# One load and product for v of four heads, f32 dummy matmuls, and batch 1's scores from pair 0 on

## The chip, the core and the metric

The kernel runs on one core of a Trainium2 chip. The core has a matrix engine (PE, with its weight loads listed as PEld), a vector engine (DVE), an activation engine (ACT), a general engine (POOL) that here issues the loads from memory, and a queue engine (SP) that here issues DMA transposes and stores. Matrix products go to an accumulation memory of eight banks, from which DVE and ACT copy them out. The metric is the time of one execution on the device in microseconds (us); the median of four runs stands for the kernel.

## The reference

Eight batches of eight heads, 1024 positions, 64 numbers a head. Keys and values are projected along the positions to 64 rows, then come attention over these 64 rows and a two-layer network on the result:

```python
k_proj = np.einsum('ks,bhsd->bhkd', E, k)
v_proj = np.einsum('ks,bhsd->bhkd', F, v)
scores = scale * np.matmul(q, k_proj.transpose(0, 1, 3, 2))
attn = softmax(scores)
x = np.matmul(attn, v_proj)            # (8, 8, 1024, 64) -> rows of 512
h = x @ w_in                           # 512 -> 2048
g = h * np.clip(h + 3.0, 0.0, 6.0) / 6.0
out = g @ w_out                        # 2048 -> 512, 8192 rows
```

All inputs and the output are f32 in memory; the kernel computes with bf16 operands and f32 sums.

## The kernel before

The program is written with its order by hand: each engine runs its instructions in the order in which the code issues them.

**Tiling.** Tokens are taken in blocks of 512 (TOK), two to a batch. Heads go in pairs j = 0 to 3: a pair is 128 columns of the model's 512. The first layer's 2048 columns are 16 groups of 128 (fo), each with four products of 128 rows (ko = the pair j), and the second layer accumulates 16 products into one output tile of 128 rows.

**PSUM tiles.** Two pools of four banks: `pmm()` and `pat()`. Each call takes the next of its four buffers, and the writer waits until the buffer's former reader is done.

**Start.** E and F come in over SP and ACT, are cast on DVE (L140) and ACT (L141), turned by eight PE transposes (L145) and copied to `e_t` and `f_t` (L147, L149). Meanwhile PE runs dummy matmuls on a constant tile of ones: `busy(n)` (L86 to L89) issues n matmuls of 128x512 bf16, into a `pmm` tile that nobody reads. There are 12 at the start (L91), two after the transposes (L151), and single ones inside the first block (L464, L467, L476). The tile `ones` also serves as the stationary operand of the sums of softmax (L255, L431).

**Loads of batch 0.** POOL issues them in this order, with a cast from f32 to bf16 on the way: four times a pair of k and half of a pair of q; then v in four loads of a pair (L113); then w_in in eight pieces (L127 to L129), the rest of q, w_out, and batch 1's k, v and q. They all go through one queue. A load waits for the load eight places before it in the list.

**First block (class First, L437 to L480).** For each pair j: `keys(j)` projects k with eight matmuls and copies the result to `kp` on DVE; `queries` transposes q; `scores(j - 1)` multiplies q and the keys of the pair before, and ACT takes the exponential (L445, one instruction for each head of the pair); `keys_transposed(j)` turns kp on PE; `sums(j)` multiplies the exponentials by ones, and ACT turns the result into 1/sum as exp(-ln) (L450, L451). `vals(j)` projects v of pair j with eight matmuls of 128 columns, and DVE (ACT for the last) copies the result to `vp` (L394). `products(j)` multiplies the weights of softmax by vp, and DVE scales the result by 1/sum into xT (L454), the first layer's input. The loop ends with pair 3's `keys_transposed`; the order behind it is lines 468 to 480: scores of pair 3, vals 0, sums 2, vals 1, products 0, sums 3, vals 2, products 1, one dummy, products 2, vals 3, then `meanwhile`, which is the first product with w_in (L169), and products 3. Then the dense work on both layers begins.

**Batch 1 (class Attention).** Its projection runs on PE at 56 us, DVE copies the keys to kp (L205), SP issues one DMA transpose of the keys to kT (L212) and two of q to qT (L157): the first fills pairs 0 and 1, the second pairs 2 and 3. A copy of one element, `mark` (L219), lets POOL go on to the next batch's loads when the first of them has landed. `visit(n)` (L332 to L361) is called for n = 0 to 3 among the groups of the second layer of batch 0's second block. `visit(0)` issues the scores of three pairs in the order 2, 0, 1 (L334), the first into two pmm tiles and the others into pat tiles, then their exponentials on ACT in the same order. `visit(1)` issues sums and values of pair 0 and the scores of pair 3; `visit(2)` sums and values of pair 1 and the sums of pair 2; `visit(3)` the rest.

From then on PE alternates between the groups of the two layers, with the attention of later batches spread among them.

Of the kernel before, what the change touches and what calls it, by code (L numbers as in the profile page):

```python
# [8 lines left out]
f32 = mybir.dt.float32  # L9
bf16 = mybir.dt.bfloat16  # L10
# [5 lines left out]
def kernel(  # L16
# [11 lines left out]
    nc = tc.nc  # L28
# [5 lines left out]
    P = 128  # L34
    SO = S // P
    KO = d_model // P
    FO = d_ff // P
    TOK = 512
# [13 lines left out]
    consts = ctx.enter_context(tc.tile_pool(name="consts", bufs=1))  # L52
# [13 lines left out]
    def pmm():  # L66
        return ps_mm.tile([P, TOK], f32, tag="mm", name="mm")

    def pat():
        return ps_at.tile([P, TOK], f32, tag="at", name="at")  # L70
# [7 lines left out]
    nc.sync.dma_start(out=ef_f32[:KP], in_=E)  # L78
    nc.scalar.dma_start(out=ef_f32[KP:], in_=F)
    nc.scalar.preload_act_table_set("natural_log_exp_and_others")  # L80
    ones = consts.tile([P, TOK], bf16, name="ones")
    nc.vector.memset(ones, 1.0)  # L82
    ident = consts.tile([P, P], bf16, name="ident")


    def busy(n):  # L86
        ps = pmm()
        for _ in range(n):
            nc.tensor.matmul(ps, ones[:, :P], ones, start=True, stop=True)  # L89

    busy(12)  # L91

    def raw_tile(name):
        return kqv_pool.tile([P, H, SO, D], bf16, tag=name, name=name)


    kqv = {0: {n: raw_tile(n) for n in ("k", "q", "v")}}
# [3 lines left out]
    def load_q0(t, hs):  # L101
        nc.gpsimd.dma_start(out=q0[:, t, hs], in_=kqv_dram["q"][0][:, hs, t * SB:(t + 1) * SB, :])  # L102

    def load_pair(n, j):
        hs = slice(2 * j, 2 * j + 2)
        nc.gpsimd.dma_start(out=kqv[0][n][:, hs], in_=kqv_dram[n][0][:, hs])  # L106

    for j in range(KO):
        load_pair("k", j)
        load_q0(0, slice(2 * j, 2 * j + 2))  # L110
        if j == 0:
            make_identity(nc, ident)
    for j in range(KO):  # L113
        load_pair("v", j)

    def load_kqv(b, order="qkv"):
        kqv[b] = {}
# [20 lines left out]
    f_t = consts.tile([P, SO, 2, KP], bf16, name="f_t")  # L138
# [9 lines left out]
    for a in range(2):  # L148
        nc.scalar.copy(f_t[:, :, a, :], ef_pv[:, 1])  # L149
    ef_t = [e_t, f_t[:, :, 0, :]]  # L150
    busy(2)  # L151

    def q_transposed(b):
# [17 lines left out]
    def rec_tile():  # L171
        return att.tile([P, 2, TOK], f32, tag="rec", name="rec", bufs=4)

    def log(rec, i, den):
        nc.scalar.activation(rec[:, i], den, AF.Ln)

    def inverse(rec, den=()):
        for i, d in enumerate(den):
            log(rec, i, d)
        flat = rec.rearrange("p i n -> p (i n)")  # L180
        nc.scalar.activation(flat, flat, AF.Exp, scale=-1.0)  # L181
# [5 lines left out]
    class Attention:  # L187
# [143 lines left out]

        def visit(self, n):  # L332
            if n == 0:
                js = 2, 0, 1  # L334
                tiles = [self.scores(j, *two) for j, two in zip(js, ((pmm, pmm), (pat, pat), (pat, pat)))]
                for j, two in zip(js, tiles):
                    self.exps(j, two)
                return lambda: None
            if n == 1:
                den, av = self.sums(0, pmm, pmm), self.values(0, pat, pat)  # L340
                last = self.scores(3, pat, pat)
                rec = rec_tile()
                inverse(rec, den)
                self.exps(3, last)
                return lambda: self.scaled(0, av, rec)
            if n == 2:
                den, av = self.sums(1, pmm, pmm), self.values(1, pat, pat)
                more = self.sums(2, pat, pat)
                rec, self.rec = rec_tile(), rec_tile()
                inverse(rec, den)  # L350
                later.extend([lambda i=i: log(self.rec, i, more[i]) for i in range(NB)])
                later.append(lambda: inverse(self.rec))
                return lambda: self.scaled(1, av, rec)
            den = self.sums(3, pmm, pat)
            early = self.values(2, pmm, pmm)
            av = self.values(3, pat, pat)
            rec = rec_tile()
            inverse(rec, den)
            self.scaled(2, early, self.rec)
            return lambda: self.scaled(3, av, rec)  # L360
# [3 lines left out]
    class First:  # L364
# [20 lines left out]
                                    self.kp[:, 2 * j + a].rearrange("p a d -> p (a d)"), ident[:KP, :KP])  # L385
            nc.vector.tensor_copy(self.kT[:, 2 * j:2 * j + 2, :].rearrange("p h m -> p (h m)"), ps)

        def vals(self, j, copy):
            ps = pat()[:, :P]
            for so in range(SO):  # L390
                nc.tensor.matmul(ps, f_t[:, so].rearrange("p a m -> p (a m)"),
                                 kqv[0]["v"][:, 2 * j:2 * j + 2, so, :],
                                 start=(so == 0), stop=(so == SO - 1))
            copy(self.vp[:, 2 * j:2 * j + 2, :].rearrange("p h d -> p (h d)"), ps)  # L394

        def queries(self, t, js):

# [39 lines left out]
        def first_block(self, meanwhile):  # L437
            recs = {}

            def scores(j):  # L440
                aT = att.tile([P, 2, HT], bf16, tag="aT0", name="aT0", bufs=KO)
                tiles = [pmm() for _ in range(2)]
                self.scores(0, j, tiles, 0)
                for r in range(2):
                    nc.scalar.activation(aT[:, r], tiles[r][:, :HT], AF.Exp, scale=scale)  # L445
                self.aT[0, j] = aT

            def sums(j):
                recs[j] = opool.tile([P, TOK], f32, tag="o_sb", name="o_sb")
                nc.scalar.activation(recs[j], self.sums(0, j, pmm), AF.Ln)  # L450
                nc.scalar.activation(recs[j], recs[j], AF.Exp, scale=-1.0)  # L451

            def products(j):
                nc.vector.tensor_mul(self.xT[:, j, 0, :], self.values(0, j, pat), recs[j])  # L454

            for j in range(KO):
                self.keys(j)
                if j > 1:
                    sums(j - 2)
                self.queries(0, (j,))  # L460
                if j > 0:
                    scores(j - 1)
                else:
                    busy(1)  # L464
                self.keys_transposed(j)
                if j < 2:
                    busy(1)  # L467
            scores(KO - 1)
            self.vals(0, nc.vector.tensor_copy)
            sums(KO - 2)  # L470
            self.vals(1, nc.vector.tensor_copy)
            products(0)
            sums(KO - 1)
            self.vals(2, nc.vector.tensor_copy)
            products(1)
            busy(1)  # L476
            products(2)
            self.vals(3, nc.scalar.copy)
            meanwhile()
            products(3)  # L480
# [103 lines left out]
    def meanwhile():  # L584
        early.append(TwoGroups(xT, 0, g[0]))
        early[0].part(0, (0,))
# [48 lines left out]
    for b in range(1, B):  # L635
# [6 lines left out]
        two, more = ((pmm, pmm), (pat, pat)), (pat, pat)  # L642
# [29 lines left out]
        for t in range(NB):  # L672
            g = g_tile()
            for fo in range(FO):
# [13 lines left out]
                n = t * SB + slots.index(fo)  # L688
# [43 lines left out]
```

## Time and profile before

| | us |
|---|---|
| median of four runs | 503.11 |
| lowest and highest | 502.77, 503.64 |
| the profiled execution's own time | 502.77 |
| its span, first to last instruction | 501.0 |
| PE busy | 494.6 |
| DVE busy | 285.3 |
| ACT busy | 239.5 |
| POOL busy | 38.7 |
| POOL's issues of v, four of them, from 7.57 | 2.91 in all |
| first issue of w_in | 10.68 |
| first product with w_in | 20.09 |

The span lies within the execution's own time; what lies around it is 502.77 - 501.0 = 1.77 us.

In an excerpt in order of time, a line gives the start, the length, the engine, the line of code, the operation, what it writes and reads, the form (partitions x elements) and, after x, how many instructions are merged into it; the square brackets give the idle time of the engine just before, and what ended it. Matmuls overlap: a new one starts before the end of the former one, so the distance of the starts is the cost of one, not its length. In a list of waits a line gives who waited for whom, the sum in us, the number of times and the longest.

### The profile page before, as it was taken

To read this page: it belongs to the slowest core of one execution; us is meant where nothing else is said; L and a number is where in the kernel's file an instruction comes from. 1 tells how busy PE (TensorE), PEld (TensorE's weight loads), DVE (VectorE), ACT (ScalarE), POOL (GpSimd) and SP (SyncE) were. 2 spreads that over 40 slices of the span, in tenths; PEclk is the share of its full clock that TensorE was granted. 3 is DMA by queue.
4 is the path that set the end of the run, shared out by engine and by line. 5 is a ranking of instruction groups with operands and counts; after the bars stand their busy time and mean duration, and the time that the engine had idled before them with its cause. 6 is when DMAs were issued, how large, how long until landed. Compare 5 with 4: busy or idle time off the path is not lost.

```text
span 501.0 us, 11177 instructions
## 1 busy us (share of the span) xinstructions
PE 494.6 (99%) x4802; PEld 256.1 (51%) x4802; DVE 285.3 (57%) x438; ACT 239.5 (48%) x414; POOL 38.7 (8%) x58
## 2 busy tenths in 40 slices
PE   8999999999999999999999999999999999999997
PEld 4554544554555545555555545555455554555554
DVE  3572736876658675666648655674755656334420
ACT  3656566665355445433564344643456344343431
POOL 8620020200020020002000020000000000000000
PEclk9999999999999999999999999999999999999999
DMA  9999999898759799549950799209411261101112
GB/s 168 198 204 207 187 174 231 150 210 176 175 95 222 174 191 215 112 113 225 207 122 22 178 195 223 73 24 232 116 43 44 59 176 44 43 22 43 44 43 84
DMA packets 83618, 68.43 MB, mean 137 GB/s; under 512 B 38256, under 2 KB 69232, under 8 KB 83568
## 3 DMA queue, kind: packets, MB, share of 16 engines
q0 software_dynamic: 32480, 29.36, 37.5%
q1 hardware_dynamic: 50864, 38.02, 30.9%
q8 instruction: 37, 0.61, 0.5%
q10 hardware_dynamic: 224, 0.33, 0.3%
q14 instruction: 13, 0.11, 0.1%
HBM read 71.83 MB, written 16.97 MB: 177 GB/s over the span
## 4 chain that ended last, share of the span: by engine, by line
PE 91%; DMA 5%; POOL 2%; SPq 1%; issue 0%; ACT 0%; DVE 0%; ACTq 0%; POOLq 0%
PE mm L169 85%; DMA qT<-q 3%; PE at L169 2%; DMA w_in_sb<-in_moe_w_in_dram 2%; PE mm L250 1%; PE at L229 1%; PE at L250 1%; PE mm L229 1%; POOL q L102 1%; POOL v L106 1%; POOL k L106 1%; SPq L212 0%; SPq L157 0%; PE at L425 0%; PE at L405 0%
## 5 line engine op out<-in xcount | busy, mean ns | idle before, releaser
L514 DVE SCALAR_TENSOR_TENSOR g<-r,mm 128x512 bf16<-128x512 f32 x256 | 174.3, 687 | 143.6 <-ACT r L513 142.9
L169 PE MATMUL mm<-w_out_sb,g 128*64 128x512 bf16 (+2 forms) x2080 | 235.6, 376 | 0.0
L169 PE MATMUL mm<-xT,w_in_sb 128*64 128x512 bf16 x2048 | 231.1, 379 | 0.2 <-DMA w_in_sb<-in_moe_w_in_dram 0.2
L513 ACT ACTIVATE r<-mm 128x512 f32<-128x512 f32 x256 | 152.7, 598 | 74.5 <-PE mm L169 73.3
L169 PEld LDWEIGHTS <-w_in_sb 128*64 128x64 bf16 x2048 | 115.7, 110 | 105.1 <-issue 0.6
L169 PEld LDWEIGHTS <-g 128*64 128x64 bf16 x2080 | 114.8, 110 | 106.5 <-issue 7.1
L548 ACT COPY o_sb<-mm 128x512 f32<-128x512 f32 x58 | 33.9, 585 | 149.9 <-PE mm L169 149.5
L270 DVE TRANSPOSE_TENSOR_REDUCE parts<-aT 128x32 f32<-128x1024 bf16 x24 | 28.8, 1226 | 0.0
L262 DVE TENSOR_TENSOR xT<-at,rec 128x512 bf16<-128x512 f32 x32 | 20.5, 683 | 8.6 <-ACT rec L181 5.8
L238 ACT ACTIVATE aT<-at 128x512 bf16<-128x512 f32 x38 | 20.7, 622 | 7.9 <-PE at L229 7.9
L262 DVE TENSOR_TENSOR xT<-mm,rec 128x512 bf16<-128x512 f32 x24 | 15.5, 686 | 7.3 <-PE mm L250 7.2
L219 POOL COPY mark<-qT 1x1 bf16<-1x1 bf16 x5 | 0.9, 177 | 202.4 <-DMA qT<-q 202.4
L205 DVE CAST kp<-at 64x512 bf16<-64x512 f32 x14 | 9.0, 678 | 11.3 <-PE at L169 11.2
L238 ACT ACTIVATE aT<-mm 128x512 bf16<-128x512 f32 x18 | 9.7, 605 | 7.6 <-PE mm L229 7.6
L169 PE MATMUL at<-k,e_t 128*64 128x512 bf16 x56 | 13.2, 379 | 0.0
L169 PE MATMUL at<-v,f_t 128*64 128x512 bf16 x56 | 13.2, 379 | 0.0
L208 DVE CAST vp<-at 64x512 bf16<-64x512 f32 x14 | 9.7, 694 | 0.4
L538 DVE COPY o_sb<-mm 128x384 f32<-128x384 f32 x1 | 0.6, 558 | 15.2 <-PE mm L169 15.2
L169 PEld LDWEIGHTS <-e_t 128*64 128x64 bf16 x56 | 6.2, 110 | 5.7
L89 PE MATMUL mm<-ones 128*128 128x512 bf16 x18 | 7.4, 549 | 1.5 <-DVE ones L82 1.5
L229 PEld LDWEIGHTS <-kT 64*64 64x64 bf16 x224 | 5.7, 106 | 5.2 <-issue 4.3
L503 DVE TENSOR_TENSOR xT<-at,rec 128x512 bf16<-128x512 f32 x4 | 2.5, 684 | 8.1 <-PE at L425 8.1
(68 smaller groups left out, 152.0 us busy)
## 6 DMA issues: line engine op xcount, KB each, us to landing
out_dram<-o_sb SPq DMA_DIRECT2D x63, 256.0 KB, 4.4
rec<-turned_rows SPq DMA_DIRECT2D x48, 256.0 KB, 6.4
k<-in_k_dram POOLq DMA_DIRECT2D x7, 1024.0 KB, 10.7
v<-in_v_dram POOLq DMA_DIRECT2D x7, 1024.0 KB, 15.7
q<-in_q_dram POOLq DMA_DIRECT2D x7, 1024.0 KB, 20.5
w_out_sb<-in_moe_w_out_dram POOLq DMA_DIRECT2D x4, 512.0 KB, 16.0
w_in_sb<-in_moe_w_in_dram POOLq DMA_DIRECT2D x5, 256.0 KB, 9.9
k<-in_k_dram POOLq DMA_DIRECT2D x4, 256.0 KB, 5.4
```

Source lines behind the costliest of these rows:

```text
L106: nc.gpsimd.dma_start(out=kqv[0][n][:, hs], in_=kqv_dram[n][0][:, hs])
L169: nc.tensor.matmul(ps[lo:lo + width], stationary[:, lo:lo + width], moving, **flags)
L205: nc.vector.tensor_copy(self.kp[:, :, a, :], self.ps[:KP].rearrange("p (h d) -> p h d", d=D))
L208: nc.vector.tensor_copy(self.vp[a * KP:(a + 1) * KP], self.ps[KP:].rearrange("p (h d) -> p h d", d=D))
L229: nc.tensor.matmul(tiles[r][t * KP:(t + 1) * KP, a * HT:(a + 1) * HT], self.kT[r * D:(r + 1) * D, 2 * j + a, :], qT[r * D:(r + 1) * D, j, ...
L238: when(lambda r=r: nc.scalar.activation(aT[:, :, r, :], tiles[r].rearrange("p (a n) -> p a n", a=2), AF.Exp, scale=scale))
L250: nc.tensor.matmul(tiles[t][c:c + D], stationary(r, 2 * j + a), self.weights(j, a)[r:r + KP], start=True, stop=True)
L262: when(lambda t=t: nc.vector.tensor_mul(self.xT[:, j, t, :], av[t], rec[:, t]))
L270: nc.vector.tensor_reduce(out=self.parts[:, j], op=ALU.add, axis=mybir.AxisListType.X, apply_transpose=True, in_=self.aT[j].rearrange("p a ...
L513: nc.scalar.activation(r, h_ps, AF.Relu, bias=0.5, scale=1.0 / 6.0)
L514: nc.vector.scalar_tensor_tensor(g[:, fo, :], r, 1.0, h_ps, op0=ALU.min, op1=ALU.mult)
L548: (copy or nc.scalar.copy)(o_sb, o_ps)
```

## The change

Four edits, in the order of the code.

1. `ones` is filled as 128x256 f32 with a number whose two halves are both the bf16 number 1; the bf16 tile `ones` is the same bytes, read as 128x512 bf16.
2. `busy(n)` multiplies f32 columns, 128 for each of the n of before, at most 256 in one matmul: `busy(12)` issues six of 256, `busy(2)` one of 256, `busy(1)` one of 128. In the instruction order an f32 matmul has no weight load of its own in front of it.
3. v of batch 0's pairs 0 and 1 comes in one load, and `vals` takes `more` pairs: `vals(0, ..., 2)` projects both pairs with eight matmuls of 256 columns and one copy. The order around it becomes: scores of pair 3, sums 2, vals 0 and 1, sums 3, products 0, vals 2, and on as before.
4. `visit(0)` scores the pairs in the order 0, 1, 2.

```diff
-    ones = consts.tile([P, TOK], bf16, name="ones")
-    nc.vector.memset(ones, 1.0)
+    ones_f32 = consts.tile([P, TOK // 2], f32, name="ones")
+    nc.vector.memset(ones_f32, 1.0 + 127 * 2.0 ** -16)
+    ones = ones_f32.bitcast(bf16)
...
     def busy(n):
         ps = pmm()
-        for _ in range(n):
-            nc.tensor.matmul(ps, ones[:, :P], ones, start=True, stop=True)
+        for lo in range(0, n * P, 2 * P):
+            m = min(2 * P, n * P - lo)
+            nc.tensor.matmul(ps[:, :m], ones_f32[:, :P], ones_f32[:, :m], start=True, stop=True)
...
-    def load_pair(n, j):
-        hs = slice(2 * j, 2 * j + 2)
+    def load_pairs(n, j, more=1):
+        hs = slice(2 * j, 2 * (j + more))
         nc.gpsimd.dma_start(out=kqv[0][n][:, hs], in_=kqv_dram[n][0][:, hs])
...
-    for j in range(KO):
-        load_pair("v", j)
+    load_pairs("v", 0, 2)
+    for j in range(2, KO):
+        load_pairs("v", j)
...
             if n == 0:
-                js = 2, 0, 1
+                js = 0, 1, 2
...
-        def vals(self, j, copy):
-            ps = pat()[:, :P]
+        def vals(self, j, copy, more=1):
+            hs = slice(2 * j, 2 * (j + more))
+            ps = pat()[:, :more * P]
             for so in range(SO):
-                nc.tensor.matmul(ps, f_t[:, so].rearrange("p a m -> p (a m)"),
-                                 kqv[0]["v"][:, 2 * j:2 * j + 2, so, :],
+                nc.tensor.matmul(ps, f_t[:, so].rearrange("p a m -> p (a m)"), kqv[0]["v"][:, hs, so, :],
                                  start=(so == 0), stop=(so == SO - 1))
-            copy(self.vp[:, 2 * j:2 * j + 2, :].rearrange("p h d -> p (h d)"), ps)
+            copy(self.vp[:, hs, :].rearrange("p h d -> p (h d)"), ps)
...
             scores(KO - 1)
-            self.vals(0, nc.vector.tensor_copy)
             sums(KO - 2)
-            self.vals(1, nc.vector.tensor_copy)
+            self.vals(0, nc.vector.tensor_copy, 2)
+            sums(KO - 1)
             products(0)
-            sums(KO - 1)
             self.vals(2, nc.vector.tensor_copy)
```

More of the change, by code (lines that the diff above doesn't have):

```diff
@@ L102, in load_q0 @@
         nc.gpsimd.dma_start(out=q0[:, t, hs], in_=kqv_dram["q"][0][:, hs, t * SB:(t + 1) * SB, :])
-    def load_pair(n, j):
-        hs = slice(2 * j, 2 * j + 2)
+    def load_pairs(n, j, more=1):
+        hs = slice(2 * j, 2 * (j + more))
         nc.gpsimd.dma_start(out=kqv[0][n][:, hs], in_=kqv_dram[n][0][:, hs])
     for j in range(KO):
-        load_pair("k", j)
+        load_pairs("k", j)
         load_q0(0, slice(2 * j, 2 * j + 2))
```

## The prediction

> **What bounds the kernel now.** I read the busy times first, then the list of what PE waited for, then PE, ACT and POOL in order of time over the first 21 us, and last the stretch around 69 us. The page's first part and PE's whole list of waits:
>
> ```profile
> PE 494.6 (99%) x4802; PEld 256.1 (51%) x4802; DVE 285.3 (57%) x438; ACT 239.5 (48%) x414; POOL 38.7 (8%) x58
> ...
> PE mm L89 <- DVE ones L82: 1.5, 1, 1.5
> PE mm L425 <- ACT aT L445: 0.6, 1, 0.6
> PE mm L229 <- DMA qT<-q: 0.4, 1, 0.4
> PE mm L418 <- DVE kT L386: 0.3, 1, 0.3
> PE mm L169 <- DMA w_in_sb<-in_moe_w_in_dram: 0.2, 1, 0.2
> ```
>
> PE is the bound: 494.6 of 501.0 us. All five waits lie before 70 us. After that PE runs without a hole, so a delay or gain of PE before 70 us arrives at the end unchanged. The change touches that stretch at two places: the first 20 us, and the wait for qT. The first, in order of time on PE:
>
> ```profile
> 1.46 5.30 PE L89 MATMUL mm<-ones 128*128 128x512 bf16 x12 [1.46 <-DVE ones L82]
> 6.55 0.86 PE L145 MATMUL at<-ident,g 128*128 128x128 bf16 x8
> 7.25 0.59 PE L89 MATMUL mm<-ones 128*128 128x512 bf16 x2
> 7.93 0.63 PE L375 MATMUL at<-k,e_t 128*64 128x128 bf16 x8
> ...
> 15.62 0.30 PE L418 MATMUL mm<-rec,kT 64*64 64x256 bf16 x4 [0.32 <-DVE kT L386]
> 15.86 0.62 PE L391 MATMUL at<-v,f_t 128*128 128x128 bf16 x8
> 16.47 0.40 PE L425 MATMUL mm<-aT,ones 64*64 64x512 bf16 x2
> 16.81 0.62 PE L391 MATMUL at<-v,f_t 128*128 128x128 bf16 x8
> 17.36 0.40 PE L425 MATMUL at<-aT,vp 64*64 64x512 bf16 x2
> ...
> 20.09 0.41 PE L169 MATMUL mm<-xT,w_in_sb 128*64 128x512 bf16 x2 [0.23 <-DMA w_in_sb<-in_moe_w_in_dram]
> ```
>
> Two speeds are to be seen. The twelve dummies start (6.55 - 1.46)/12 = 0.424 us apart; the two at 7.25 start 0.21 apart. PE starts at half speed, and the single records put the turn at 6.98 us, inside the eight transposes. (The granted clock reads 1.00 throughout; it doesn't show this.) At the end of the stretch PE comes to the first w_in product 0.23 us before its weights: that DMA is the cap on any gain here, and a delay beyond 0.23 us passes through. What ACT does meanwhile, and when loads land, by POOL, which waits on each load issued eight before:
>
> ```profile
> 15.78 1.19 ACT L445 ACTIVATE aT<-mm 128x256 bf16<-128x256 f32 x4
> ...
> 15.88 0.74 POOL L125 DMA_DIRECT2D w_in_sb<-in_moe_w_in_dram  x1 [0.54 <-DMA v<-in_v_dram]
> ```
>
> The four exponentials are pair 2's and pair 3's, about 0.28 apart; pair 2's weights are complete at about 16.4. The POOL row is released by v's second pair (its semaphore is full at 15.59; the first pair's at 14.30). The second place:
>
> ```profile
> 67.35 0.18 POOL L219 COPY mark<-qT 1x1 bf16<-1x1 bf16 x1 [36.45 <-DMA qT<-q]
> 69.14 0.41 PE L229 MATMUL mm<-qT,kT 64*64 64x256 bf16 x8 [0.42 <-DMA qT<-q]
> 69.36 0.63 PE L229 MATMUL at<-qT,kT 64*64 64x256 bf16 x16
> ```
>
> The mark is copied out of qT's first half (pairs 0 and 1, landed 67.30). PE stands until the second half lands at 69.00, since pair 2 is scored first.
>
> **The change part by part.** Times are against the profiled execution (span 501.0, time 502.77, the lowest of the four; the median is 0.34 higher). I add the sum to the median.
>
> *The memset.* 0.48 us for 128x512 bf16; the new one has half the elements and the same bytes: 0.24 to 0.48. The dummies start up to 0.24 earlier. The transposes behind them can't start before their inputs, whose cast on ACT ends at 6.18 (0.37 before they do). I take -0.12, bounds -0.24 and 0.
>
> *The twelve dummies become six of 256 f32 columns.* No f32 matmul is in this trace, so bounds. Low: f32 columns stream like bf16 ones, 256 in half of 0.427, all six in 1.28 us. High: each takes four passes with the weights of each loaded in the open, 4 x (0.213 + 0.151, the slow weight load of ones) = 1.46, six in 8.7. The middle is 5.0 against 5.09 now, and I take 0. At the high end the transposes start at 10.0 instead of 6.55: +3.4. At the low end PE would stand from 2.7 to 6.2, and the price is the slow clock (third rival).
>
> The Trainium skill ("FP8 and Floating Point Precision", TensorE Precision Notes) says that true FP32 is four passes through the array; that makes 6 x 4 x 0.213 = 5.12, an estimate, and no change. Its page "TensorE: Matmul & The Clock Gate" (Weight-path perf modes) speaks against the edit: the fast weight load is not used for FP32. The rows here show 0.095 to 0.151 us for bf16 weights of 128 columns; by the rule f32 weights would cost more, which leans to the high end.
>
> *The two dummies at 7.25* become one of 256 columns: by the same middle 0.43, ending near 7.7. Keys start at 7.93 behind DVE's e_t copy, which covers 0.25; uncovered only at the high end (+0.3).
>
> *The four single dummies.* One at 8.73 has 0.19 us of cover (the next PE work waits for kp until 9.14). One at 9.30, one at 10.99 and one at 18.59 stand in the line of work, 0.216 us each at full speed. Their f32 form of 128 columns: low 0.056 (the spacing of 128 bf16 columns), high 4 x (0.056 + 0.095) = 0.60, middle 0.33: +0.11 each, +0.33 for three; bounds -0.48 and +1.15.
>
> *v's first two pairs in one load and one product.* POOL issues three v loads instead of four, 0.73 us saved before the w_in issues. Nothing is gained: the first w_in piece is issued at 10.68 and lands at 20.05, behind the same bytes. Every later load now waits for the load one place further back in the list, again in front of a full queue. The merged load lands with v's second pair, about 15.6, and its product isn't reached before 16.8. The product is 8 matmuls of 256 columns at 0.109 (between 0.056 for 128 and 0.216 for 512) in place of 16 at 0.056: about 0.05 saved with a tile switch. The copy to vp becomes one of 128x256, 0.42 by the line through 0.29 (128x128) and 0.69 (64x512).
>
> *The order around it.* Now vals(0) runs in the time that sums(2) waits for ACT. Afterwards sums(2) comes directly behind the last scores, at 15.86, and waits to 16.45 with all of PE's work queued behind it: the merged vals, sums(3), every product. The wait of 0.6 has lost its cover. From there: sums(2) 0.34, so vals at 16.79; eight matmuls and the switch 0.99, sums(3) at 17.78; the last vals result is out at 17.87, DVE copies to 18.31, products(0) at 18.37 instead of 17.36, with PE idle 0.26. Then today's spacings: products 0.34, vals(2) 0.55, products(1) 0.34, dummy 0.32, products(2) 0.34, vals(3) 0.55: the first w_in product at 20.8 against 20.09. The last product follows at 21.2 against 20.43. I take +0.75, bounds +0.5 (DVE's copy as short as 0.29) and +0.9. DVE and ACT get later by no more: the sums of pair 3 reach ACT 0.1 later, and xT's last piece, 22.3, comes before PE asks for it at 22.6.
>
> *Batch 1 scores pair 0 first.* Pairs 0 and 1 need the half landed at 67.30, so they start at 68.64 (the usual 0.31 after the last product) and fill the stall; pair 2, at 69.08, still waits 0.06. Same tiles, same number of exponentials on ACT; pair 2's weights are now ready third, at about 73, and its sums come at 77. Gain 0.43, bounds 0 (if the half is as late as the whole) and 0.49. SP's order is unchanged: the transposes are issued behind kp, which comes from PE, and shift with it.
>
> **The sum:** -0.12 + 0 + 0.33 + 0.75 - 0.43 = +0.53, so 503.11 + 0.53 = 503.6. That is 0.1%; a difference up to 0.2% (1.0 us) I count as no change, as little more can be told apart in this kernel.
>
> **The rivals.**
> 1. *The f32 dummies are long (slower).* The 256-column one costs over 0.93 us instead of 0.85 and the single ones nearer their high end. For: an f32 matmul has no separate weight load in the instruction order, so it may not be fetched ahead as the bf16 one is. Against: nothing in the rows. Weights half in the open, slow: 4 x (0.213 + 0.076) = 1.16, six in 6.9, +1.7 at the transposes; the turn of the clock at 6.98 takes back about 0.3; the single ones are in the sum. That gives +1.9 and 505.0. It decides from +0.47 beyond the sum.
> 2. *No loss from the order.* If sums(2) weren't held, the w_in landing at 20.05 stays the gate, and only the 0.43 and about 0.15 of the rest remain: 502.6. Against: the ACT row.
> 3. *PE stays slow (slower).* If the f32 stream is short or doesn't bring the clock up as 5.5 us of bf16 did, the stretch from 6.98 on runs at half speed for some 3 us longer. Each group of eight 128-column matmuls then costs 0.41 more; four of them: +1.6 beside the sum, 505.2.
> 4. *The weights come sooner (faster).* The first w_in piece needs 1.9 us after v's last landing (18.15) where 256 KB pieces come every 1.3. If one load fewer let it land at 19.4, and the order cost nothing: -0.65 - 0.43 = 502.0. Against: the bytes ahead of it are the same.
>
> **How the numbers follow.** Forecast 0.37, its own range 503.0 to 504.1 (copy, single dummies); rival 1 0.31, rival 2 0.11, rival 3 0.13, rival 4 0.08. Faster 0.08 (rival 4), slower 0.44 (1 and 3), within 0.2% 0.48. The range takes rival 2 below, and above the prices of 1 and 3: 502.5 to 505.3.
>
> **What would show it.** In the changed trace: the transposes still start near 6.5 and turn to 0.056 spacing near 7; sums(2) waits about 0.6 for ACT; the first w_in product is at 20.8 with no wait for its DMA; the scores of batch 1 have no stall over 0.1. It is wrong if the six f32 dummies take less than 4 or more than 5.6 us, if eight matmuls of 128 columns take 1 us after 8 us, or if w_in lands after PE asks for it.

## The result and the profile after

| | before | after |
|---|---|---|
| median, us | 502.83 (70 executions) | 503.71 (47 executions) |
| lowest and highest, us | 501.93, 505.03 | 502.31, 504.80 |
| ratio to before | | 1.0017, 95% interval 1.0012 to 1.0021 |
| span of the profiled execution, us | 501.0 | 500.9 |

The change costs 0.9 us: less than the 0.2% that was set as the bound of no change, but clear of the interval. The profiled execution after the change is one of the shorter ones (502.65), and its trace alone would tell nothing of a loss. The page's first part and the list of PE's waits, after:

```profile
PE 494.2 (99%) x4798; PEld 258.6 (52%) x4798; DVE 285.0 (57%) x437; ACT 239.6 (48%) x414; POOL 38.0 (8%) x57
...
PE mm L93 <- DVE ones L83: 1.2, 1, 1.2
PE mm L430 <- ACT aT L450: 1.2, 2, 0.6
PE at L150 <- ACT g L146: 0.5, 1, 0.5
PE mm L423 <- DVE kT L391: 0.3, 1, 0.3
PE at L430 <- DVE vp L399: 0.2, 1, 0.2
```

Of the five waits of before, those for qT and for w_in are gone. In their place PE waits a second time for ACT's weights (sums(2)), once for ACT's cast of F (the transposes) and once for DVE's vp (the first product). PE in order of time, after:

```profile
1.19 4.32 PE L93 MATMUL mm<-ones 128*128 128x256 f32 x12 [1.19 <-DVE ones L83]
6.01 0.71 PE L150 MATMUL at<-ident,g 128*128 128x128 bf16 x8 [0.50 <-ACT g L146]
6.55 0.65 PE L93 MATMUL mm<-ones 128*128 128x256 f32 x2
7.23 0.63 PE L380 MATMUL at<-k,e_t 128*64 128x128 bf16 x8
...
8.60 0.49 PE L93 MATMUL mm<-ones 128*128 128x128 f32 x2
9.02 0.63 PE L380 MATMUL at<-k,e_t 128*64 128x128 bf16 x8
...
15.12 0.30 PE L423 MATMUL mm<-rec,kT 64*64 64x256 bf16 x4 [0.32 <-DVE kT L391]
15.96 0.40 PE L430 MATMUL mm<-aT,ones 64*64 64x512 bf16 x2 [0.55 <-ACT aT L450]
16.30 1.05 PE L397 MATMUL at<-v,f_t 128*128 128x256 bf16 x8
17.28 0.40 PE L430 MATMUL mm<-aT,ones 64*64 64x512 bf16 x2
17.87 0.40 PE L430 MATMUL at<-aT,vp 64*64 64x512 bf16 x2 [0.18 <-DVE vp L399]
...
20.39 0.41 PE L174 MATMUL mm<-xT,w_in_sb 128*64 128x512 bf16 x2
...
69.03 0.41 PE L234 MATMUL mm<-qT,kT 64*64 64x256 bf16 x8
```

Each f32 matmul is recorded as two. The six take 4.32 us here, because PE's clock rose at 4.18 us instead of 7.03 (the trace's record of the clock); PE then stands 0.5 us for the cast of F. From the transposes to the first w_in product it is now 20.39 - 6.01 = 14.38 us, against 20.09 - 6.55 = 13.54 before: 0.84 more. The early start hides most of it in this execution. The scores at 69.03 have no wait.

What the one trace hides, the list of all executions shows. For each the mean granted clock of TensorE is known. After the change, the profiled execution counted in, 22 of 48 have 0.999 or 1.000, with a median of 503.00, and 26 have 0.996 or 0.997, with a median of 504.09 (the two medians are 1.09 apart). Of the 85 executions of the kernel before that ran beside the experiments, one lies below 0.999. A clock of 0.9965 over 502 us is 1.75 us lost, as much as half speed for some 3.5 us.

### The profile page after: what moved, and what is told of

Read it like the earlier page. It is cut to its first block, busy times and chain, and to the rows that moved or that the text cites. A ratio compares the mean times of both kernels' runs of the same rounds, so it can differ in the third digit from the quotient of the medians.

```text
span 500.9 us, 11167 instructions
## 1 busy us (share of the span) xinstructions
PE 494.2 (99%) x4798; PEld 258.6 (52%) x4798; DVE 285.0 (57%) x437; ACT 239.6 (48%) x414; POOL 38.0 (8%) x57
## 4 chain that ended last, share of the span: by engine, by line
PE 96%; DMA 2%; ACT 1%; issue 0%; DVE 0%; SPq 0%; ACTq 0%
PE mm L174 88%; PE at L174 2%; DMA qT<-q 1%; PE mm L255 1%; DMA g<-in_F_dram 1%; PE at L234 1%; PE at L255 1%; PE mm L234 1%; PE at L430 1%; PE at L397 0%; PE mm L93 0%; PE at L380 0%; PE at L410 0%; ACT o_sb L456 0%; ACT o_sb L455 0%; PE mm L430 0%
## 5 line engine op out<-in xcount | busy, mean ns | idle before, releaser
L93 PE MATMUL mm<-ones 128*128 128x256 f32 (+1 forms) x22 | 6.9, 443 | 1.2 <-DVE ones L83 1.2
```

The costliest lines, as they stand in the source:

```text
L93: nc.tensor.matmul(ps[:, :m], ones_f32[:, :P], ones_f32[:, :m], start=True, stop=True)
```

## The experiments

Each kernel ran beside the kernel before on the same chip. "Full clock" counts executions at 0.999 or 1.000.

| kernel | median, us | before beside it, us | ratio (95%) | full clock |
|---|---|---|---|---|
| e1: memset and f32 dummies alone | 504.63 | 502.79 | 1.0037 (1.0025 to 1.0049) | 5 of 5 |
| e2: v's load, product and order alone | 504.37 | 502.79 | 1.0035 (1.0023 to 1.0048) | 4 of 6 |
| e3: order of batch 1's scores alone | 503.04 | 502.79 | 1.0008 (0.9999 to 1.0016) | 12 of 12 |
| e4: all but the memset and f32 dummies | 504.07 | 502.79 | 1.0020 (1.0009 to 1.0031) | 5 of 10 |
| e5: changed kernel, v's product first | 502.85 | 503.12 | 1.0002 (0.9993 to 1.0010) | 12 of 12 |
| e6: dummies for the hole, behind ACT | 506.66 | 503.12 | 1.0075 (1.0063 to 1.0087) | 0 of 5 |
| e7: before, twice as many bf16 dummies | 503.15 | 503.12 | 1.0007 (0.9999 to 1.0016) | 11 of 11 |
| e8: e3, spread sums loaded by POOL | 502.94 | 503.12 | 1.0006 (0.9994 to 1.0019) | 10 of 11 |
| e9: e1 once more | 504.70 | 503.03 | 1.0032 (1.0022 to 1.0042) | 11 of 12 |
| e10: e5 with bf16 dummies | 503.26 | 503.03 | 1.0002 (0.9993 to 1.0011) | 12 of 12 |
| e11: dummies in the hole | 503.83 | 503.03 | 1.0011 (1.0002 to 1.0020) | 11 of 11 |
| e12: e10, spread sums loaded by POOL | 504.59 | 503.03 | 1.0041 (1.0014 to 1.0067) | 5 of 12 |

### The parts one by one (e1 to e4)

My first theory was that the f32 dummies make the clock fall; the rival was the hole that the new order leaves in PE's work. e1 takes the memset and `busy` from the changed kernel, e3 the one line `js = 0, 1, 2`, e4 all but the memset and `busy`, and e2 is e4 without e3's line.

> Only the memset and the dummies of the change. Theory (the clock): the changed kernel's executions fall into two groups, 22 with a granted clock of 0.999 or 1.000 (median 503.0 us) and 26 with 0.996 or 0.997 (median 504.1); f32 dummies make the second group. Then some third to two thirds of this kernel's executions show 0.996 or 0.997, those about 1.1 us longer than the others, and the others are 502.6 to 503.0, since w_in's landing at 20.05 us caps what an earlier start gains. Rival (the holes): the clock falls because the new order leaves PE idle at 15.5 and 17.6 us; then this kernel shows 1.000 in nearly all executions and stays at 502.6 to 503.0.

> Only the merged load and product of v and the order around it. Theory (the clock goes with the f32 dummies): granted clock 1.000 in nearly all executions; sums(2) waits 0.55 us for ACT, the first w_in product comes 0.7 us later than before, at 20.8, and the time is 503.5 (502.83 + 0.7). Rival (the holes): a third to two thirds of the executions at 0.996 or 0.997 and the median near 504.

> Only batch 1's scores in the order 0, 1, 2. Both theories: no wait for qT at 69 us, 0.43 us gained, 502.4, clock 1.000. If the wait only moves on to pair 2 or returns later, 502.8.

> The changed kernel with the bf16 memset and bf16 dummies of before. Theory (the clock goes with the f32 dummies): 1.000 in nearly all executions, 502.83 + 0.7 - 0.43 = 503.1. Rival (the holes): the same two groups of clocks as the changed kernel, median 503.7 or more.

My theory fell. The f32 dummies alone kept the clock (5 of 5); the order without f32 lost it in 7 of 16 executions. The profiled execution of e2 shows where. First PE in order of time, then the busy time of the engines in two stretches of 3.4 us (the stretch, its length, the engines' busy times with the instructions in brackets, PEclk the granted clock):

```profile
15.71 0.30 PE L421 MATMUL mm<-rec,kT 64*64 64x256 bf16 x4 [0.32 <-DVE kT L389]
16.57 0.64 PE L428 MATMUL mm<-aT,ones 64*64 64x512 bf16 x2 [0.55 <-ACT aT L448]
17.14 1.89 PE L395 MATMUL at<-v,f_t 128*128 128x256 bf16 x8
...
13.20:16.60 3.40, 1.92 (x26) 1.12 (x24) 1.26 (x5) 2.88 (x8) 1.72 (x3) 0.99 1.24 205
16.60:20.00 3.40, 3.40 (x14) 1.37 (x13) 0.42 (x1) 2.06 (x5) 1.54 (x3) 0.50 1.54 191
```

The eight matmuls of v take 1.89 us where the changed kernel's profile has 1.05. From 16.6 to 20.0 the granted clock is 0.50. In the 3.4 us before that, PE was busy for 1.92 (56%). The same stretch of the kernel before:

```profile
13.20:16.60 3.40, 2.47 (x33) 1.59 (x30) 1.25 (x6) 2.88 (x9) 2.41 (x4) 1.00 1.23 203
```

There PE is busy 2.47 us of 3.40. It waited 0.61 and 0.32 us in this region already; the change adds 0.55.

The other readings missed too. e3 gained nothing where 0.43 was hoped for (that the wait might return later stood beside it), and e1 lost 1.8 us with a full clock, where at most 0.2 was expected. Both are taken up below. e2 was put at 503.5 without a fall of the clock; its four executions at full clock have a median of 503.97.

### The hole, taken away, filled and made larger (e5, e6, e11)

e5 puts the merged product into ACT's time, where the single one stood:

```diff
+            self.vals(0, nc.vector.tensor_copy, 2)
             sums(KO - 2)
-            self.vals(0, nc.vector.tensor_copy, 2)
             sums(KO - 1)
```

> The changed kernel (f32 dummies and all) with the merged product of v moved ahead of sums(2), into ACT's time, as vals(0) stood before. Theory now (holes on PE let the clock fall): PE has no wait at 15.4 us, the granted clock is 1.000 in nearly all executions, the first w_in product comes as soon as its weights allow (within 0.3 us of the landing), and the time is 502.4 to 503.0: that of before, since qT's landing at 183.5 us takes any gain. Rival (the f32 dummies lose the time, as they did alone): 503.5 or more.

The clock stayed full in 12 of 12, and the kernel is as fast as before. The product of 256 columns runs from 15.88 to 16.86, and PE has no wait between the scores of pair 3 and the w_in product.

e6 was meant to fill the hole and made it larger. It writes four bf16 dummies of 256 columns to the unused half of the last scores' tile (`spare`, returned by `scores`), ahead of sums(2):

```diff
-            scores(KO - 1)
+            spare = scores(KO - 1)
+            for _ in range(4):
+                nc.tensor.matmul(spare[:, HT:], ones[:, :P], ones[:, :HT], start=True, stop=True)
             sums(KO - 2)
```

> The changed kernel with four bf16 dummies of 256 columns (0.44 us) in PE's wait ahead of sums(2). No product is moved, so PE's lateness stays (first w_in product within 0.1 us of the changed kernel's 20.4). Theory (holes): the granted clock is 0.999 or 1.000 in at least nine of ten executions and the median falls to about 503.0, that of the changed kernel's executions at full clock. Rival (the clock falls for another reason, the f32 dummies or the length of the product): still a third to two thirds of the executions at 0.996 or 0.997, median 503.7.

The tile's reader on ACT had to end first, so PE stood twice as long:

```profile
17.22 0.60 PE L476 MATMUL mm<-ones 128*128 128x256 bf16 x4 [1.10 <-ACT aT L450]
17.75 0.40 PE L430 MATMUL mm<-aT,ones 64*64 64x512 bf16 x2
18.08 1.89 PE L397 MATMUL at<-v,f_t 128*128 128x256 bf16 x8
```

In this trace the granted clock is 0.50 from 18.02 to 21.43, and in the 3.41 us ahead of that PE was busy for 2.00 (59%). The clock fell in five executions of five. The hole was not filled; as a larger dose of it, the run speaks for the theory. e11 writes the same dummies to a tile of the other pool:

```diff
             scores(KO - 1)
+            spare = pat()
+            for _ in range(4):
+                nc.tensor.matmul(spare[:, :HT], ones[:, :P], ones[:, :HT], start=True, stop=True)
             sums(KO - 2)
```

> The changed kernel with the four bf16 dummies (0.44 us) ahead of sums(2) written to a tile of the other pool, whose last reader is long done, so that they run in the wait and not behind ACT as in the first attempt (which made the hole 1.10 us, and the clock fell in five of five). The first w_in product stays within 0.1 us of where it was beside its transposes. Theory (holes): clock 0.999 or 1.000 in nearly all executions, median 502.8 to 503.2. Rival (something else in the changed order): a third or more at 0.996 or 0.997, median 503.7.

Now the dummies run in the wait, and sums(2) follows without one:

```profile
15.90 0.30 PE L423 MATMUL mm<-rec,kT 64*64 64x256 bf16 x4 [0.32 <-DVE kT L391]
16.13 0.61 PE L476 MATMUL at<-ones 128*128 128x256 bf16 x4
16.75 0.41 PE L430 MATMUL mm<-aT,ones 64*64 64x512 bf16 x2
...
13.20:16.70 3.50, 2.58 (x30) 1.57 (x29) 1.44 (x6) 2.95 (x8) 1.83 (x3) 1.00 1.25 210
```

The clock is full in 11 of 11, with every product where the changed kernel has it: 14.39 us from transposes (6.78) to w_in (21.17). That settles the cause of the clock's fall. The time expected for it missed: 503.83, not 502.8 to 503.2. What is left, 1.0011 (0.55 us), is put down to the lateness of PE itself; no run shows that alone. The clock's part of the loss is therefore 0.3 us by this comparison ((1.0017 - 1.0011) x 503, the intervals overlap) and 26/48 x 1.09 = 0.6 by the changed kernel's own executions; nearer it can't be told.

Why the same hole costs one execution its clock and not another can be seen in the traces. The trace records when the granted clock changes, and in each the changes are whole multiples of 3.41 us apart: in e2 it rises at 6.32, falls at 16.56 (three times 3.41 later) and rises again at 19.98; in e12 it rises at 6.74 and falls at 187.65, 53 times 3.41 later. So the clock is set in steps of 3.41 us, and since the first rise lies anywhere from 4.18 to 7.33 in the fourteen traces, the steps lie differently to the work each time. PE's busy time in the steps that matter:

| trace | step, us | PE busy, of 3.41 us | granted clock in the next step |
|---|---|---|---|
| e2 | 13.15 to 16.56 | 1.94 | 0.50 |
| e4 | 13.90 to 17.31 | 2.06 | 0.50 |
| e6 | 14.61 to 18.02 | 2.00 | 0.50 |
| e12 | 184.24 to 187.65 | 1.16 | 0.50 |
| e12 | 126.20 to 129.62 | 2.03 | 1.00 |
| e9 | 181.81 to 185.22 | 2.32 | 1.00 |
| after | 14.42 to 17.83 | 2.40 | 1.00 |

The changed kernel's own profile has a stretch as empty as that of e2 (12.60 to 16.00: 1.93 of 3.40), but the edge of a step at 14.42 cuts it in two, and the clock stayed. The border lies near 2.0 of 3.41 and isn't sharp (2.03 kept the clock, 2.00 lost it). In the profiles without the hole (before, e1, e3, e5, e7, e9, e10, e11) no stretch of 3.41 us from 8 to 20 us holds less than 2.48. That half of the executions lose it doesn't follow from these figures alone.

### Where a gain of PE goes (e3, e8, e12)

The wait that e3 takes away at 69 us comes back at 183. The scores of a later batch in the kernel before, and in e3:

```profile
183.23 0.39 PE L250 MATMUL at<-aT,vp 64*64 64x512 bf16 x4
183.71 0.41 PE L229 MATMUL at<-qT,kT 64*64 64x256 bf16 x8
```

```profile
182.55 0.39 PE L250 MATMUL at<-aT,vp 64*64 64x512 bf16 x4
183.41 0.41 PE L229 MATMUL at<-qT,kT 64*64 64x256 bf16 x8 [0.47 <-DMA qT<-q]
```

PE comes 0.68 us earlier, but qT lands at 183.37 in e3 and at 183.67 before (the semaphore is full then), so 0.30 of it is left. Before, this was no wait in the list, since the row ahead ends only 0.09 us before PE goes on. But the two rows start 0.48 apart there, and 0.22 in e8 below, where nothing holds PE: some 0.26 us were waited already. SP's queue in order of time shows why the landing doesn't follow PE (before):

```profile
165.96 6.08 SPq L293 DMA_DIRECT2D rec<-turned_rows  x8
172.13 1.01 SPq L549 DMA_DIRECT2D out_dram<-o_sb  x2
173.70 1.70 SPq L212 DMA_TRANSPOSE kT<-kp  x1
175.53 5.91 SPq L157 DMA_TRANSPOSE qT<-q  x2
```

Eight loads of the spread sums stand ahead of the transposes, and they can't start before rows that land at 165.9 together with the last of three large loads of k, v and q (165.60). In e3 POOL issued these loads 0.67 us earlier and SP the rows 0.68, yet the loads end at 165.57 and the rows land at 165.91. e8 lets POOL issue the eight loads (`nc.gpsimd.dma_start` for `nc.sync.dma_start` in `spread_sums`), with e3's line.

> The kernel before with batch 1's scores in the order 0, 1, 2 and the eight loads of the spread sums of each batch issued by POOL, not SP. Theory (the 0.43 us gained at 69 us are lost again at 183.4, where qT lands late because SP issues its transposes only after eight such loads, 166 to 172 us): the transposes are issued some 3 us earlier, PE doesn't wait for qT at 183, and the 0.43 arrive with the 0.2 that the kernel before waits there: 502.2 to 502.4. Rival (the transposes are late because the memory traffic of these loads slows them, whoever issues them): the wait at 183 stays, 502.8 or more.

The transposes went out at 171.62 instead of 173.18 in e3, qT landed at 181.34, and the wait at 183 is gone. The time did not fall beyond the interval: in the profiled execution PE waited 0.72 us for v's last load at 19 us, and 0.3 at 126 us for DVE, which waits for the same spread sums. Whether the 0.43 would arrive without these is open. e12 combines this with e10:

> The kernel with v's product first and bf16 dummies, and POOL issuing the loads of the spread sums: no wait for qT at 69 and at 183. If these two were all that stood between the change and a gain: 502.2 or less. If DVE's wait for those loads at 122 to 126 us, or a fetch of instructions on v's last load, takes their place, as in the kernel with POOL's loads alone: 502.6 to 503.0.

It lost. In its profiled execution PE waited 1.4 us for DVE at 126.5 and 2.2 us for qT behind the rows at 184.7, and the clock fell behind the second wait too (0.50 from 187.65 to 191.06). No version that I ran is faster than the kernel before.

### The dummies (e1, e7, e9, e10)

A single f32 dummy of 128 columns adds 0.10 to the line of work: 8.60 to 9.02 in the changed profile, 9.30 to 9.62 before. Three of these are 0.3 us, and e1 lost 1.8. The trace of e1 holds one fetch of instructions in the first 25 us (16 KB, a queue of its own), at 16.55 us; before it is at 17.98. In both, the transfer then under way ends on its last part of sixteen 1.6 to 1.7 us behind its first, where v's loads ahead of it take 0.3 to 0.4. Before, that is w_in's first piece; in e1 v's third load, for which PE waits 0.42. e7 tests the fetch without f32: `busy` issues 2n bf16 matmuls of 256 columns.

> The kernel before with twice as many bf16 dummies of half the columns: the same time on PE, 18 more weight loads and matmuls. Theory (the one 16 KB fetch of instructions in the first 25 us, at 17.98 before and at 16.55 and 15.79 with the f32 dummies, is made when an engine has come so far in its program, and holds back the transfer under way by about 1.3 us): the fetch comes earlier than 17.5, v's second or third load lands with its last part 1 us behind the first, and PE waits for v: +0.3 to +1.0, 503.1 to 503.8. Rival (only f32 moves the fetch, or it does no harm): the fetch at 17.5 to 18.0, v on time, 502.8.

The fetch moved as expected, to 15.52, and v's third load was late on one part (16.35 to 18.03). But PE asked for it at 17.9 and lost 0.2; in time e7 is not told apart from before, though its profile also has a wait of 0.8 for DVE at 126 us. So a fetch on v's load is not the whole of e1. e9 repeats e1:

> The memset and the f32 dummies alone, once more, since the first five executions gave +1.8 us and nothing in the profile accounts for more than 0.7 to 1.0 (three single dummies 0.1 longer each, a wait of 0.42 for v's third load behind the fetch of instructions, a late start). Theory: +0.3 to +1.0, 503.1 to 503.9, clock 1.000. Rival (f32 dummies cost more than the profile shows): 504.4 or more again. If it was chance: 502.8 to 503.1.

The loss is real. Its profile has the wait for v (0.56) and a larger one at 183:

```profile
18.36 0.62 PE L393 MATMUL at<-v,f_t 128*128 128x128 bf16 x8 [0.56 <-DMA v<-in_v_dram]
...
185.38 0.41 PE L231 MATMUL at<-qT,kT 64*64 64x256 bf16 x8 [1.25 <-DMA qT<-q]
```

Following it back: POOL starts the loads of k, v and q only when a transpose to kT has landed. POOL in order of time, before and in e9:

```profile
143.47 0.18 POOL L219 COPY mark<-kT 1x1 bf16<-1x1 bf16 x1 [44.72 <-DMA kT<-kp]
```

```profile
145.35 0.18 POOL L221 COPY mark<-kT 1x1 bf16<-1x1 bf16 x1 [46.23 <-DMA kT<-kp]
```

SP issued that transpose at 140.72 before and at 141.25 in e9, 0.5 us apart, but the last of its sixteen parts was in at 142.39 and at 144.68, which in e9 is 1.9 us behind the first (142.75). The fetch is at 143.05 before, after the last part, and at 142.86 in e9, between first and last (in e1 at 143.39, with the last part at 145.21). The loads then end at 168.28 instead of 165.60, and qT lands at 185.34. In the changed kernel the last part was in at 142.27, on time. In the other twelve traces no fetch falls between the first and last part of this transpose, and these are 0.2 to 0.6 us apart; in e1 and e9 they are 1.9 to 2.0. So the reading rests on traces; no run was made that moves this fetch alone.

e10 asks what f32 costs in a good order:

> The changed kernel with the merged product of v ahead of sums(2) and with bf16 dummies in the lengths of before; only the memset stays f32. Theory (the hole takes the clock, the f32 dummies cost little in this order): clock 1.000, 502.5 to 502.9, within 0.3 us of the same kernel with f32 dummies (502.85). Rival (the f32 dummies cost 1 us or more whatever the order): 501.9 or less.

Nothing that can be measured: 1.0002 with f32 (e5) and 1.0002 with bf16, each to about 0.0009. The time expected for e10, 502.5 to 502.9, was missed by 0.4 us; the kernel before beside it was at 503.03.

## Why the prediction came out right, and where it was wrong

The forecast was 503.6 and no change beyond 0.2%; 503.71 was measured, 0.9 us slower against 0.5 forecast (part of the nearness is the base, 502.83 by seventy executions against 503.11 by four). The wait behind the new order and its length were right, but the sum lacked a term, the clock, and one of its steps holds only in part. That the number came out so near is partly luck, and how much can't be told: by e11 the lateness is 0.55, as in the sum, with 0.3 of the clock on top; by the changed kernel's own executions at full clock it is 0.2 (503.00 against 502.83), and the clock makes up the rest.

- **Memset:** 0.27 us instead of 0.48, and PE starts at 1.19 instead of 1.46, a little beyond the bound of -0.24. What it brings depends on F: the transposes started at 6.0 to 7.0 us in the profiles of all kernels, mostly behind the cast of F. The changed kernel's is the earliest, 0.54 before that of the kernel before, where 0.12 was taken.
- **Twelve dummies as six:** right. Two records of 0.427 each at half speed make 0.853, against 0.85 for two of before; the prediction had it as the middle of two far bounds. FP32 as four passes through the array, as the Trainium skill ("FP8 and Floating Point Precision", TensorE Precision Notes) has it, agrees. What the six take in all hangs on when the clock rises: 4.32 us here, with the rise at 4.18, and 5.49 in e1, at 6.97. The prediction took the turn at 6.98 as given.
- **Single dummies:** +0.10 each, +0.11 was taken. Their two weight loads, 0.19 us each, would fill nearly all of the 0.42: the lean to the high end that the rule on fast weight loads gave fits for 128 columns and didn't show for 256.
- **The order:** right, and with the wait of 0.55 where it was put. From the scores of pair 3 to the first w_in product it is 20.39 - 15.12 = 5.27 us, against 20.09 - 15.62 = 4.47 before: 0.80, or 0.70 without the 0.10 of the one dummy in it. The chain worked out gave 20.8 - 20.09 = 0.71.
- **Scores from pair 0:** the stall at 69 us went, as predicted. That a gain of PE before 70 us "arrives at the end unchanged" doesn't hold for e3, where it is the only change: qT at 183 lands by a chain of loads and not by PE. The trace of before had it: its chain of waits goes through a qT landing at 183.67, with PE at 183.71. I read the list of PE's waits, where this wait doesn't stand, and passed over the chain. In the changed kernel, where the new order has made PE late, the 0.43 may well count: PE is 0.30 later than before at w_in (20.39 against 20.09) and 0.11 earlier at the scores (69.03 against 69.14), and the span is 0.1 shorter (500.9 against 501.0). e2 and e4 differ by this line alone, and e4 is the shorter (504.07 against 504.37; at full clock 503.35 of five executions against 503.97 of four). That is too few to show it.
- **What the sum left out:** the clock. The prediction saw the wait of 0.6 lose its cover and priced it as 0.6 us of time, not as idleness that makes the next 3.4 us run at half speed in half of the executions. Rival 3 had a slow PE, at 1.6 us where 1.09 was measured, but for the wrong reason, a short f32 stream. The Trainium skill ("TensorE: Matmul & The Clock Gate", the goals in the section on why this matters for kernels) advises against idle gaps over about 3 us. Here no single gap passed 0.61 us in e2 and 1.10 in e6; a step of 3.41 us with PE busy 57 to 60% was enough (e2, e4, e6), while in all fourteen traces every step with 67% or more kept the clock. The measurement decides.
- **Rival 1** (long f32 dummies) was not met: their own price was the middle value. What it had for it, no weight load in front of an f32 matmul, is so in the program's order only: the changed profile has 22 weight loads to the 22 records. The 1.8 us of e1 came, as far as the traces show, by another way. **Rivals 2 and 4** were not met either: sums(2) was held, and w_in's first piece landed at 19.88.

## What to carry to other kernels

Before work is moved out of a wait, count how busy the engine stays over the next few microseconds, not only how long the new wait is; a half-filled stretch can cost the clock of the next one. Read the chain of waits for landings that come just in time: they can be missing from the list of waits and can take away a gain made before them. And look at the granted clock of all executions before one profile is believed.

## What was not expected of the hardware

- The clock is set in steps of 3.41 us. It fell to half for one step after a step with PE busy 1.94 us (e2), 2.06 (e4) or 2.00 (e6), and stayed full after 2.32 (e9), 2.40 (after) and once 2.03 (e12). With the smaller hole it fell in 33 of 64 executions (after, e2, e4), with the larger in 5 of 5, and without it in 2 of 160 (before, e1, e3, e5, e7, e9, e10, e11). e8 and e12, where other waits come in, are left out: 1 of 11 and 7 of 12.
- An f32 matmul of 256 columns takes 0.853 us at half speed and 0.43 at full; one of 128 columns still 0.42.
- The transfer that is under way at a fetch of 16 KB of instructions ends on its last part 1.6 to 2.0 us behind its first, against 0.2 to 0.7 for v's loads ahead of it and for the transposes that no fetch meets. The Trainium skill ("Runtime: NRT & Kernel Launch", Instruction fetch mechanics) has such fetches in blocks of 16 KiB on a queue of the sequencer's own, mostly hidden. In these traces they are not hidden from the transfers, and the time of the first (15.52 in e7, 17.98 before) moves with the dummies in the program, and with it the load that is hit.
